# Linear attention and a gated FFN on one core: the first batch's q by casting loads, the remainder tile's product in quadrants, the third batch's sums three slots later

## The chip, the core and the metric

One core of a Trainium2 chip runs the kernel. TensorE (PE) multiplies, VectorE (DVE), ScalarE (ACT) and GpSimd (POOL) work element by element, and SyncE (SP), ACT and POOL issue transfers (DMAs). The metric is the device time of one execution in microseconds: the median of the runs.

## What is computed

```python
# attention part, per batch and head: q, k, v are (8 batches, 8 heads, 576 rows, 64)
kv = np.einsum('bhsd,bhse->bhde', k, v)
out = np.einsum('bhsd,bhde->bhse', q, kv)
rms = np.sqrt(np.mean(out * out, axis=-1, keepdims=True) + 1e-06)
attn = out / rms * g_norm
# FFN part on 4608 tokens of 512: w_gate, w_val (512, 1536), w_out (1536, 512)
x = attn.transpose(0, 2, 1, 3).reshape(4608, 512)
xn = x / np.sqrt(np.mean(x * x, axis=-1, keepdims=True) + 1e-06) * rms_g
g = xn @ w_gate
y = (g / (1 + np.exp(-g)) * (xn @ w_val)) @ w_out
```

All inputs and the output are float32; the kernel multiplies in bfloat16.

## The kernel before

Each batch has 576 rows. 512 of them are the main part, handled as four chunks of 128 (`MAIN`, `NC`); the 64 left over are the remainder (`REM`). Two batches' remainders form one tile of 128 rows, and the eight remainders together make one more token group of 512 for the FFN. So the FFN runs over nine groups of 512 tokens, in the order 0 to 6, the remainders, 7.

A group's FFN is a row of slots. A gate slot (`gate_of`, `mm1`) multiplies x by 128 columns of `w_gate` into a PSUM tile of the pool `mm1` (three buffers), and ACT takes its silu (line 703). A val slot does the same with `w_val`, and DVE multiplies it by the silu into h (line 712). After 12 pairs, the output slots (`slots_b`) multiply h by `w_out` into the PSUM pool `o2` (two buffers), ACT copies the tile to `osb` and SP stores it. Attention work of the next batch is laid between these slots. The PSUM pool `att` has three buffers.

Two ways set the order of the work. From the third batch on, a `Placer` walks the slots, and puts each operation into the first slot with room, by listed costs and by what it depends on (`place_attention`). Each engine then executes its instructions strictly in the order in which they stand. In `place_attention` PE makes kv and then o (`o_heads`: lines 367 to 378, 64-row matmuls that use the two row halves of the array); ACT squares o (`sq_`) and copies it (`outa_`); POOL multiplies the square by the squared gain (`wsq`); DVE sums both over each head (`red`, line 473), turns the sums into one factor per row and head (`chain`, twelve short steps) and scales the rows (`xna_`); SP transposes them to x by DMA (`x_dma`). The third, fourth, sixth and eighth batches also handle the remainder tile of two batches (`o_rem`, eight matmuls with 128 rows of weights, line 362).

The first batch, lines 820 to 996, is written out by hand. The loads: POOL issues loads that cast to bfloat16 on the way, first v (`load_cast`), then `w_gate` and `w_val` in four pieces each (`load_w`). A POOL load waits until the one eight before it has landed. SP and ACT issue plain loads: k in two halves of four heads, then q's first two chunks in 512-byte pieces. q's last two chunks are issued by SP and ACT behind the landing of v's remainder (line 838). DVE, ACT and POOL cast what came as float32 (`cast_main`).

The first half of the tokens (chunks 0 and 1) takes the shortest way. `kv_pairs` makes kv for two heads at a time (a pair, index j; `P0` are pairs 0 and 1, `P1` are 2 and 3) and DVE masks it (line 304). `qT_mm` transposes q on PE (line 316) and ACT and DVE copy it out (line 338). `oT_mm` (line 423) makes the transposed o, ACT squares it (line 434), `stat_pairs` sums the squares by matmul (line 448). `lead_chain` makes the factor: four DVE steps, a square root on ACT (line 497), the load of the silu table on ACT (line 498), a reciprocal on DVE (line 499). Meanwhile `o_pairs` makes o itself (line 390), DVE scales it (`xna_pairs`, line 400), PE transposes it (line 571), and ACT and DVE copy it to x with the gain (lines 581 and 583). Then come 22 early slots over these 256 tokens, `gates` (line 722) first. `spin` (line 245) fills PE's waits with matmuls on zeros.

`behind(n)` puts the second half's attention behind early slot n: transposes of q at 0, oT at 2 and 3, sums at 5, the chain at 5 to 9, o at 7 and 8, scaling at 11 and 12, transposes of x at 14 and 15. After 19 of the early slots, three slots over the second 256 tokens follow, and then the last three early ones.

Of the kernel before, what the change touches and what calls it, by code (L numbers as in the profile page):

```python
# [87 lines left out]
def kernel(  # L88
# [17 lines left out]
    NC = 4  # L106
# [17 lines left out]
    sq_p = pool("sq", 3)  # L124
# [64 lines left out]
    def load_cast(b, t, heads=None):  # L189
        to = qc if t == 0 else (vc if t == 2 else kc)[b % 2]  # L190
        if heads is None:
            if t == 0:
                to = q01r[b * REM : (b + 1) * REM]
            else:
                to = to[:REM, :, NC * D :]
            return nc.gpsimd.dma_start(
                out=to, in_=src[t][b, :, MAIN:S, :].rearrange("h p d -> p h d")
            )
        view = src[t][b, :, 0:MAIN, :].rearrange("h (p c) d -> p h (c d)", c=NC)[:, heads[0] : heads[1]]
        return nc.gpsimd.dma_start(out=to[:, heads[0] : heads[1], : NC * D], in_=view)  # L200

# [48 lines left out]
    class Att:  # L250
# [61 lines left out]
        def qT_mm(self, js, chunks, pool=None):  # L312
            qT_ps = (pool or att_p).tile([128, len(js), len(chunks) * 128], BF16, name="o2" if pool else "att")
            for n, j in enumerate(js):
                for i, c in enumerate(chunks):
                    nc.tensor.matmul(
                        qT_ps[:, n, i * 128 : (i + 1) * 128], lhsT=self.pair(0, c, j), rhs=ident, is_transpose=True,
                        start=True, stop=True, skip_group_check=True,
                    )
            return qT_ps  # L320
# [34 lines left out]
        def o_rem(self):  # L355

            self.o[NC] = o = att_p.tile([128, H, D], FP32, name="att")
            of = (kvs[2], kvs[1]) if self.b == 2 else (kvs[0], kvs[1])
            for j in range(NS):
                for n in range(2):  # L360
                    at = slice(n * REM, (n + 1) * REM)
                    nc.tensor.matmul(  # L362
                        o[at, 2 * j : 2 * j + 2, :], lhsT=self.qTj[:, j, NC, at], rhs=of[n][:, j, :, :],
                        start=True, stop=True, skip_group_check=True,
                    )

        def o_heads(self):

            for n, (pool_, name) in enumerate(((o2_p, "o2"), (o2_p, "o2"), (att_p, "att"), (att_p, "att"))):
                self.o["main", n] = pool_.tile([128, 2, H // 2, D], FP32, name=name)  # L370
            for c in range(NC):
                for j in range(NS):
                    for half in range(2):
                        rows = slice(half * D, (half + 1) * D)
                        nc.tensor.matmul(  # L375
                            self.o["main", c // 2 * 2 + half][:, c % 2, j, :], lhsT=self.qTj[rows, j, c, :],
                            rhs=self.kv[rows, j, half, :], start=True, stop=True, skip_group_check=True,
                        )

# [237 lines left out]
    def place_attention(P, b, casts=(), at=0, chain_at=0):  # L617
# [9 lines left out]
        main = P.psum(0.73, a.o_heads, kv + qt, 2)  # L627
        for c in N1:
            p = P.psum(0.3, a.o_rem, kv + qt) if c >= NC else main
            s = P.put("ACT", 0.6, lambda c=c: a.sq_(c), [p])  # L630
            outs[c] = P.put("ACT", 0.6, lambda c=c: a.outa_(c), [p])
            if c >= 2:
                P.tiles[-1 if c >= NC else c - 4] += [s, outs[c]]
# [99 lines left out]
    def rows_of(g, t):  # L733

        if g < B:
# [88 lines left out]
    v_loads = [G.dma_start(out=vr[: REM // 2].rearrange("p h c d -> p h (c d)"), in_=two(2))]  # L824
    v_loads += [load_cast(0, 2, hsx) for hsx in (H0, H1)]
    load_main(0, 1, H0)
    load_main(0, 1, H1, queue=A)
    load_main(0, 0, cs=(0, 2))
    krst = stage.tile([128, H, NC * D], FP32, name="stg")[: REM // 2, :, : 2 * D]
    A.dma_start(out=krst, in_=two(1))  # L830
# [5 lines left out]
    for hsx, queue in ((H0, nc.sync), (H1, A)):  # L836
        rest = load_main(0, 0, hsx, cs=(2, 4), queue=queue)
        tc.add_manual_dep(rest.ins, v_loads[0].ins.name, SYNC, reason="k and v have the queues first")

    make_identity(nc, ident)  # L840
    make_identity(nc, identf)
    w_loads = [load_w(n) for n in range(len(FB))]
    G.memset(kvs[0], 0.0)
    G.memset(kvs[1], 0.0)
    for tile_ in (kc[0], kc[1], vc[0], vc[1]):
        G.memset(tile_[REM:, :, NC * D :], 0.0)
# [7 lines left out]
    spin(mm1_p.tile([128, MAIN], FP32, name="mm1"), 18)  # L854
# [4 lines left out]
    cast_main(0, 0, V, cs=(0, 2))  # L859
    kva = a.kv_pairs(P0, 4)  # L860
    qa, qb = (a.qT_mm(js, (0, 1)) for js in (P0, P1))
    gT = o2_p.tile([128, NS + 1], FP32, name="o2")
    nc.tensor.matmul(gT, lhsT=grow, rhs=identf, is_transpose=True, start=True, stop=True, skip_group_check=True)
    kvb = a.kv_pairs(P1)
    for i, j in enumerate(P0):
        a.kv_pairs_out(kva, i, j)
    a.qT_out(qa, P0, 0, A)
    a.qT_out(qb, P1, 0, V)
# [5 lines left out]
    ta = a.oT_mm(P0, 0, 2, o2_p)  # L874
    a.sqT_(ta, P0, 0, 2)
    for i, j in enumerate(P1):
        a.kv_pairs_out(kvb, i, j)
# [3 lines left out]
    for i, j in enumerate(P1):  # L881
        a.sqT_(a.oT_mm((j,), 0, 2, (o2_p, mm1_p)[i], 4 * (1 - i)), (j,), 0, 2)
# [10 lines left out]
    for j, pool_, eng in zip(ALL, (o2_p, o2_p, None, None), (A, V, A, V)):  # L893
        a.xT_mm((j,), (0, 1), pool_)
        a.xT_out(j, (0, 1), eng)

    for hsx in (H0, H1):
        cast_main(0, 0, G, hsx, cs=(2, 4))
    for t in (0, 2, 1):
        load_cast(1, t, (0, H))  # L900
        if t:
            load_cast(1, t)
    wo_loads = [load_wo(n) for n in range(NF // OB)]
# [12 lines left out]
    steps = {5: (0, 4), 7: (4, 6), 8: (6, 8), 9: (8, 12)}  # L916

    def behind(n):
        if n == 0:
            ps = a.qT_mm(ALL, (2, 3))  # L920
            a.qT_out(ps[:, 0:2], P0, 2, V)
            a.qT_out(ps[:, 2:4], P1, 2, V)
        elif n in (2, 3):
            js = (P0, P1)[n - 2]
            a.sqT_(a.oT_mm(js, 2, 4, o2_p), js, 2, 4)
        elif n == 5:
# [6 lines left out]
        if n in (7, 8):  # L933
            held[n - 7] = a.o_pairs((P0, P1)[n - 7], 2, 4, att_p, "att")
        if n in (11, 12):
            i = (11, 12).index(n)
            a.xna_pairs(held[i], (P0, P1)[i], 2, 4)
        elif n in (14, 15):
            i = (14, 15).index(n)
# [47 lines left out]
    cut = len(early) - FB[-1]  # L987
# [37 lines left out]
```

## Time and profile before

| | us |
|---|---|
| median of 3 runs | 321.6 (321.56 to 321.62) |
| the profiled execution | 321.76 |
| its span, first to last instruction | 320.0 |
| PE busy in the span | 312.8 |
| DVE, ACT, POOL busy | 169.2, 138.0, 85.2 |

The profile shows the one execution that was traced; its own time stands 0.16 us above the median. Its page gives the busy time of each engine and the span in 40 slices of 8 us. PE's row of slices begins 8 7 9, and is 9 (90% or more) from there up to the last slice, where it is 5. Work on PE includes the filler matmuls, so a busy PE isn't always useful. Other views of the trace used below are the chain of work that ended last in order of time, the timeline of instructions (start, length, engine, line, operation, number of instructions, and in brackets the idle time before the first and what ended it), and windows, which give the busy time of each engine in a stretch and the bytes that the DMAs wrote.

### The profile page before, as it was taken

What the parts mean: (1) busy time and instruction counts of PE and PEld (TensorE: products, weight loads), DVE (VectorE), ACT (ScalarE), POOL (GpSimd) and SP (SyncE); (2) the same over time, 40 slices, a digit from 0 to 9 for tenths busy, and PEclk for the clock granted to TensorE, in tenths of its full rate; (3) what the DMA queues carried; (4) which work ended last, traced back from release to release, by engine and by line L of the source; (5) the groups of instructions that cost most, each with busy time, mean ns of one, the idle gap of its engine ahead of it and who ended that gap; (6) DMA issues with size and microseconds to landing.
All of it is one profiled execution on the core that took longest, in us unless ns stands there. A gap on an engine that the chain in (4) does not pass through costs nothing.

```text
span 320.0 us, 5497 instructions
## 1 busy us (share of the span) xinstructions
PE 312.8 (98%) x2122; PEld 157.7 (49%) x2122; DVE 169.2 (53%) x381; ACT 138.0 (43%) x254; POOL 85.2 (27%) x105
## 2 busy tenths in 40 slices
PE   8799999999999999999999999999999999999995
PEld 3578865444444444444544444444444444444443
DVE  4565536589749651955186717571778043203410
ACT  1465454596667314632383228322842233223321
POOL 8653430077017400830075007500510000000000
PEclk9999999999999999999999999999999999999999
DMA  8999999999761974498349875964000600040002
GB/s 210 221 203 199 195 231 205 228 209 135 153 197 53 166 155 137 131 166 153 121 128 133 148 153 145 153 127 137 11 3 10 183 21 2 15 107 12 0 33 98
DMA packets 79253, 40.69 MB, mean 127 GB/s; under 512 B 42872, under 2 KB 74748, under 8 KB 79228
## 3 DMA queue, kind: packets, MB, share of 16 engines
q0 software_dynamic: 31200, 14.22, 35.1%
q1 hardware_dynamic: 46544, 25.14, 32.2%
q10 hardware_dynamic: 1484, 0.99, 1.0%
q8 instruction: 16, 0.26, 0.3%
q14 instruction: 9, 0.07, 0.1%
HBM read 37.78 MB, written 9.44 MB: 148 GB/s over the span
## 4 chain that ended last, share of the span: by engine, by line
PE 91%; DMA 8%; issue 0%; DVE 0%; ACT 0%; POOLq 0%
PE mm L694 57%; PE o L729 27%; DMA wv<-in_moe_w_val_dram 5%; DMA remv<-in_v_dram 2%; PE att L281 2%; PE mm L729 2%; PE o L375 1%; PE att L375 0%; PE att L362 0%; PE mm L756 0%; PE o L756 0%; PE att L571 0%; PE att L327 0%; PE att L423 0%; PE att L350 0%
## 5 line engine op out<-in xcount | busy, mean ns | idle before, releaser
L712 DVE TENSOR_TENSOR h<-silu,mm 128x512 bf16<-128x512 bf16 (+1 forms) x120 | 75.5, 631 | 86.9 <-PE mm L694 77.0
L703 ACT ACTIVATE silu<-mm 128x512 bf16<-128x512 f32 (+1 forms) x120 | 66.4, 556 | 86.4 <-PE mm L694 75.3
L694 PE MATMUL mm<-x,wv 128*128 128x512 bf16 (+1 forms) x432 | 99.9, 356 | 0.2 <-DMA wv<-in_moe_w_val_dram 0.2
L694 PE MATMUL mm<-x,wg 128*128 128x512 bf16 (+1 forms) x420 | 97.9, 358 | 0.0
L729 PE MATMUL o<-wo,h 128*128 128x512 bf16 x396 | 90.1, 379 | 0.0
L694 PEld LDWEIGHTS <-wv 128*128 128x128 bf16 x480 | 46.2, 98 | 45.7 <-DMA wv<-in_moe_w_val_dram 0.5
L694 PEld LDWEIGHTS <-wg 128*128 128x128 bf16 x468 | 45.1, 98 | 45.7 <-DMA wg<-in_moe_w_gate_dram 0.2
L465 POOL TENSOR_TENSOR sq<-sq,g 128x512 bf16<-128x512 bf16 x28 | 32.0, 1154 | 129.0 <-ACT sq L410 129.0
L729 PEld LDWEIGHTS <-h 128*128 128x128 bf16 x420 | 40.3, 98 | 46.5
L745 ACT COPY osb<-o 128x512 f32<-128x512 f32 x33 | 19.3, 587 | 69.1 <-PE o L729 69.1
L473 DVE TENSOR_REDUCE st<-sq 128x8 f32<-128x512 bf16 x56 | 35.9, 678 | 0.2
L310 DVE CAST kvs<-att 64x256 bf16<-64x256 f32 x14 | 5.9, 422 | 31.9 <-PE att L281 31.7
L540 DVE TENSOR_TENSOR xna<-outa,al 128x512 bf16<-128x512 bf16 x24 | 15.0, 683 | 0.0
L694 PE MATMUL mm<-xr,wg 128*128 128x512 bf16 x48 | 12.3, 379 | 0.0
L694 PE MATMUL mm<-xr,wv 128*128 128x512 bf16 x48 | 12.3, 379 | 0.0
L216 POOL CAST main_q<-stg 128x1024 bf16<-128x1024 f32 (+1 forms) x12 | 11.4, 996 | 1.1 <-DMA stg<-in_q_dram 1.1
L245 PE MATMUL mm<-idle 128*128 128x512 bf16 x27 | 9.0, 505 | 1.2 <-DVE idle L138 1.2
L410 ACT ACTIVATE sq<-att 128x512 bf16<-128x512 f32 x16 | 9.8, 615 | 0.0
L414 ACT CAST outa<-att 128x512 bf16<-128x512 f32 x16 | 9.6, 600 | 0.0
L850 ACT ACTIVATE wv<-wv,gain 128x384 bf16<-128x384 bf16 x16 | 9.0, 608 | 0.4 <-PE mm L694 0.4
L200 POOL DMA_DIRECT2D vc<-in_v_dram x9 | 7.8, 872 | 1.1 <-PE mm L694 1.1
L729 PE MATMUL mm<-wo,h 128*128 128x512 bf16 x24 | 7.8, 379 | 0.0
(132 smaller groups left out, 175.1 us busy)
## 6 DMA issues: line engine op xcount, KB each, us to landing
out_dram<-osb SPq DMA_DIRECT2D x31, 256.0 KB, 2.5
stg<-in_q_dram SPq DMA_DIRECT2D x6, 1024.0 KB, 7.5
vc<-in_v_dram POOLq DMA_DIRECT2D x7, 512.0 KB, 8.2
kc<-in_k_dram POOLq DMA_DIRECT2D x7, 512.0 KB, 6.2
wg<-in_moe_w_gate_dram POOLq DMA_DIRECT2D x4, 384.0 KB, 14.9
wv<-in_moe_w_val_dram POOLq DMA_DIRECT2D x4, 384.0 KB, 16.3
wo<-in_moe_w_out_dram POOLq DMA_DIRECT2D x4, 384.0 KB, 14.7
out_dram<-osb SPq DMA_DIRECT2D x9, 128.0 KB, 2.3
```

The costliest lines, as they stand in the source:

```text
L216: return copy(out=mains[b, t][:, cs[0] : cs[1], h0:h1, :], in_=staged[b, t].rearrange("p h (c d) -> p c h d", c=NC)[:, cs[0] : cs[1], h0:h ...
L245: nc.tensor.matmul(ps, lhsT=idle[:, :128], rhs=idle[:, : ps.shape[-1]], start=True, stop=True, skip_group_check=True)
L410: nc.scalar.activation(out=self.sq[c][:, 0], in_=self.o_of(c), func=ACT.Square)
L414: nc.scalar.copy(out=self.outa[c], in_=self.o_of(c))
L465: eng.tensor_tensor(out=self.sq[c][:, 1], in0=self.sq[c][:, 0], in1=g2, op=OP.mult)
L473: nc.vector.reduce_sum(out=self.part(self.st[:, which], c), in_=of, axis=AX.X)
L540: return eng.tensor_tensor(out=self.part(self.xna, c), in0=self.outa[c].rearrange("p (c h) d -> p c h d", c=2), in1=self.part(self.al, c). ...
L694: nc.tensor.matmul(ps[:, : c1 - c0], lhsT=w[n][:, s, jj * 128 : (jj + 1) * 128], rhs=x_of(g, s, c0, c1), start=s == 0, stop=s == NS - 1)
L703: nc.scalar.activation(out=sis[g, j][:, c0:c1], in_=ps, func=ACT.Silu)
L712: nc.vector.tensor_tensor(out=hs[g, j][:, c0:c1], in0=sis[g, j][:, c0:c1], in1=v_ps, op=OP.mult)
L729: nc.tensor.matmul(ps, lhsT=hs[g, j][:, t * 128 : (t + 1) * 128], rhs=wo[j // OB][:, j % OB, :], start=j == 0, stop=j == NF - 1)
L745: (eng.copy if eng is nc.scalar else eng.tensor_copy)(out=o, in_=ps)
```

## The change

The first batch's q comes in four casting loads on POOL's queue, two for each half of the tokens, one for heads 0 to 3 into partitions 0 to 63 and one for heads 4 to 7 into partitions 64 to 127. A piece is 1024 bytes. The first two stand between the halves of v, of which the second is split in two; the other two stand behind v and behind the identity matrices, ahead of the weights. k comes in four quarters on SP and ACT, and k's remainder moves from ACT to SP. The float32 q loads and their casts are gone. The tokens' order inside the first batch changes with it, so that each of its output tiles is stored in two halves (`rows_of`). `qT_quads` transposes q in 64x64 pieces. kv of the pairs 2 and 3 is made one pair at a time.

The second half's q is transposed and copied out before the first gates, and its oT made there; the rest of its attention moves from early slots 5 to 15 to early slots 0 to 9. The three slots over the second 256 tokens stand after 13 early slots instead of 19. POOL's memsets of kvs, kc and vc move behind the loads of the second batch.

In the batches with a remainder tile, `o_rem` runs right behind `o_heads` as sixteen 64x64 matmuls into two PSUM tiles, one of `att` and one of `mm1`, for the even and the odd heads; ACT squares and copies each in halves, first of all chunks. For the third batch the DVE sums of the weighted squares are placed three slots later. The pool `sq` has four buffers instead of three.

```diff
+    def load_q0(part):
...
+        for hh in range(2):
+            nc.gpsimd.dma_start(
+                out=mains[0, 0][hh * D : (hh + 1) * D, part],
+                in_=q[0, hh * H // 2 : (hh + 1) * H // 2, part * MAIN // 2 : (part + 1) * MAIN // 2, :].rearrange(
+                    "h (p c) d -> p h (c d)", c=NC
+                ),
+            )
...
-        def qT_mm(self, js, chunks, pool=None):
...
+        def qT_quads(self, part, halves, pools):
+            tiles = [
+                pool.tile([128, 2, MAIN // 2], BF16, name="o2" if pool is o2_p else "att") for pool in pools
+            ]
+            for c in range(NC):
+                for h in range(H // 2):
+                    for ps, hh in zip(tiles, halves):
+                        rows, at = slice(hh * D, (hh + 1) * D), slice(h % 2 * D, (h % 2 + 1) * D)
+                        nc.tensor.matmul(
+                            ps[at, h // 2, c * D : (c + 1) * D],
+                            lhsT=mains[0, 0][rows, part, h, c * D : (c + 1) * D], rhs=ident[rows, rows],
+                            is_transpose=True, start=True, stop=True, skip_group_check=True,
+                        )
...
         def o_rem(self):
 
-            self.o[NC] = o = att_p.tile([128, H, D], FP32, name="att")
             of = (kvs[2], kvs[1]) if self.b == 2 else (kvs[0], kvs[1])
+            self.o[NC] = [
+                pool_.tile([128, H // 2, D], FP32, name=name) for pool_, name in ((att_p, "att"), (mm1_p, "mm1"))
+            ]
             for j in range(NS):
                 for n in range(2):
                     at = slice(n * REM, (n + 1) * REM)
-                    nc.tensor.matmul(
-                        o[at, 2 * j : 2 * j + 2, :], lhsT=self.qTj[:, j, NC, at], rhs=of[n][:, j, :, :],
-                        start=True, stop=True, skip_group_check=True,
-                    )
+                    for half in range(2):
+                        rows = slice(half * D, (half + 1) * D)
+                        nc.tensor.matmul(
+                            self.o[NC][half][at, j, :], lhsT=self.qTj[rows, j, NC, at],
+                            rhs=of[n][rows, j, half, :], start=True, stop=True, skip_group_check=True,
+                        )
...
+        rem = a.chunks - NC
+        main = P.psum(0.73 + 0.25 * rem, a.o_heads, kv + qt, 2 + rem)
+        for c in (*N1[NC:], *N1[:NC]):
+            if c == NC:
+                for n in (1, 0):
+                    s = P.put("ACT", 0.38, lambda n=n: a.sq_rem(n), [main])
+                    outs[c] = P.put("ACT", 0.38, lambda n=n: a.outa_rem(n), [main])
...
-            reds.append(P.put("DVE", 0.68, lambda c=c: a.red(c, 1), [w]))
+            reds.append(P.put("DVE", 0.68, lambda c=c: a.red(c, 1), [w], w[1] + 3 * (b == 2)))
...
+    load_cast(0, 2, H0)
+    load_q0(0)
+    load_cast(0, 2, (4, 6))
+    load_cast(0, 2, (6, 8))
+    for n, queue in enumerate((nc.sync, A, nc.sync, A)):
+        load_main(0, 1, (2 * n, 2 * n + 2), queue=queue)
...
+    load_q0(1)
     w_loads = [load_w(n) for n in range(len(FB))]
...
+    kva = a.kv_pairs(P0)
...
+    qa, qb = a.qT_quads(0, (0, 1), (att_p, att_p))
+    a.qT_out(qa, P0, 0, A)
+    a.qT_out(qb, P1, 0, V)
...
+    kvc = a.kv_pairs((2,))
+    ta = a.oT_mm(P0, 0, 2, o2_p)
...
+    kvd = a.kv_pairs((3,))
+    a.sqT_(a.oT_mm((2,), 0, 2, o2_p), (2,), 0, 2)
+    a.kv_pairs_out(kvd, 0, 3)
...
+    a.sqT_(a.oT_mm((3,), 0, 2, None, 2), (3,), 0, 2)
     a.stat_pairs(P0, 0, 2, mm1_p, "mm1", guard=True)
+    ox = a.o_pairs(P0, 0, 2, att_p, "att")
+    (la,) = a.qT_quads(1, (0,), (o2_p,))
+    a.qT_out(la, P0, 2, A)
     a.stat_pairs(P1, 0, 2, mm1_p, "mm1")
-    ox = a.o_pairs(P0, 0, 2, att_p, "att")
     oy = a.o_pairs(P1, 0, 2, att_p, "att")
+    (lb,) = a.qT_quads(1, (1,), (att_p,))
+    a.qT_out(lb, P1, 2, A)
     a.lead_chain(0, 2)
-    spin(mm1_p.tile([128, MAIN], FP32, name="mm1"), 5)
+    a.sqT_(a.oT_mm(P0, 2, 4, o2_p), P0, 2, 4)
+    xt = [a.xT_ps(1, (0, 1), pool_) for pool_ in (o2_p, o2_p, None, None)]
+    lo = a.oT_mm(P1, 2, 4)
+    spin(mm1_p.tile([128, MAIN], FP32, name="mm1"), 3)
...
+    for j in ALL:
+        a.xT_mm((j,), (0, 1), ps=xt[j])
+        a.xT_out(j, (0, 1), A if j == 2 else V)
+    a.sqT_(lo, P1, 2, 4)
...
-    steps = {5: (0, 4), 7: (4, 6), 8: (6, 8), 9: (8, 12)}
+    steps = {0: (0, 4), 1: (4, 6), 2: (6, 8), 3: (8, 12)}
...
-    cut = len(early) - FB[-1]
+    cut = 1 + 2 * FB[0] + FB[1] + FB[2]
```

More of the change, by code (lines that the diff above doesn't have):

```diff
@@ L123 @@
     outa_p = pool("outa", 6)
-    sq_p = pool("sq", 3)
+    sq_p = pool("sq", 4)
     stat = pool("stat", 2)
@@ L310, in kv_half @@
             nc.vector.tensor_copy(out=self.kv[rows, :, half, :], in_=self.kv_ps[rows, :, cols])
-        def qT_mm(self, js, chunks, pool=None):
[L313 to L317, printed above, removed]
-                        start=True, stop=True, skip_group_check=True,
-                    )
-            return qT_ps
+        def qT_quads(self, part, halves, pools):
[11 more added lines that the diff above has]
+                        )
+            return tiles
         def qT_heads(self, js, chunks):
@@ L733, in rows_of @@
     def rows_of(g, t):
+        if g == 0:
+            n = MAIN // 2
+            view = out[t // 2 * n : (t // 2 + 1) * n, :].rearrange("(p c) d -> p c d", c=NC)
+            return [(slice(i * D, (i + 1) * D), view[:, t % 2 * 2 + i, :]) for i in range(2)]
         if g < B:
@@ L823 @@
     ALL = range(NS)
[L824 to L828, printed above, removed]
+    G.dma_start(out=vr[: REM // 2].rearrange("p h c d -> p h (c d)"), in_=two(2))
+    load_cast(0, 2, H0)
[4 more added lines that the diff above has]
+        load_main(0, 1, (2 * n, 2 * n + 2), queue=queue)
     krst = stage.tile([128, H, NC * D], FP32, name="stg")[: REM // 2, :, : 2 * D]
-    A.dma_start(out=krst, in_=two(1))
+    nc.sync.dma_start(out=krst, in_=two(1))
     A.preload_act_table(ACT.Sqrt)
```

92 lines of the change are left out of this document (41 added, 51 removed).

## The prediction

> **What bounds the kernel now.** I read the page's busy shares, then the chain of waits in order of time, then the timeline of the first 32 us, and last the windows.
>
> ```profile
> PE 312.8 (98%) x2122; PEld 157.7 (49%) x2122; DVE 169.2 (53%) x381; ACT 138.0 (43%) x254; POOL 85.2 (27%) x105
> ```
>
> PE is nearly always busy, but filler counts as busy (27 spins of 512 columns, line 245). The chain shows where that matters:
>
> ```profile
> 1.31 7.23 DMA remv<-in_v_dram
> 8.54 0.28 issue
> 8.82 17.15 DMA wv<-in_moe_w_val_dram
> 25.98 0.05 issue
> 26.02 1.05 PE mm L694 x8
> ...
> 316.45 0.02 issue
> 316.47 0.27 ACT osb L764
> ```
>
> From 26 us on there is one unbroken run of PE work up to 316.45; before it, loads. So only three things move the end: when the first useful gate burst finishes, how much PE work lies behind it, and any hole in that run. The start:
>
> ```profile
> 9.07 1.04 ACT L216 CAST main_k<-stg 128x1024 bf16<-128x1024 f32 x1 [5.90 <-DMA remv<-in_v_dram]
> 10.43 0.38 PE L297 MATMUL mm<-vc,main_k 128*128 128x128 bf16 x4 [1.48 <-DMA vc<-in_v_dram]
> 11.52 0.59 ACT L338 COPY qTs<-att 128x512 bf16<-128x512 bf16 x1 [1.41 <-PE att L316]
> ...
> 14.42 0.26 DVE L491 RECIPROCAL r<-mm 128x16 f32<-128x16 f32 x1 [0.84 <-PE mm L448]
> 15.33 0.22 ACT L497 ACTIVATE nt<-z 128x16 f32<-128x16 f32 x1 [1.23 <-DVE z L494]
> 15.57 1.28 ACT L498 ACT_TABLE_LOAD   x1
> 15.58 0.25 DVE L499 RECIPROCAL al<-nt 128x16 f32<-128x16 f32 x1 [0.28 <-ACT nt L497]
> 15.95 1.42 DVE L400 TENSOR_TENSOR xna<-att,al 128x256 bf16<-128x256 f32 x4
> 17.54 1.47 PE L722 MATMUL mm<-x,wg 128*128 128x256 bf16 x12
> 18.84 0.94 ACT L703 ACTIVATE silu<-mm 128x256 bf16<-128x256 f32 x3 [0.95 <-PE mm L722]
> 18.85 0.61 PE L316 MATMUL att<-ident,main_q 128*128 128x128 bf16 x8
> ```
>
> PE waits 1.48 us for v; the chain of sums then runs 14.42 to 15.83 and the scaled rows (xna) to 17.37. The first gate burst ends at 18.84: call that G. Between G and 27.93, where the last hole closes, the instructions' own lengths (0.108 us per 256 columns) add to 8.5 of 9.1 us, so 0.6 us of holes.
>
> **The change, part by part.** The sum is made on the profiled execution: last PE work at 316.47, span 320.0, 321.76 in all, 0.16 above the median of 321.6.
>
> *Work taken out of the run behind G.* The second half's eight transposes of q (18.85 to 19.25, 0.40) and its four oT matmuls (20.17 to 20.39 and 20.83 to 21.05, 0.44) move ahead of G, into time where PE waits or spins. Gain 0.84. Uncovered, they cost it back, so 0 to 0.84.
>
> *Holes behind G.* The second half's sums now stand behind early slots 0 to 3 instead of 5 to 9. DVE gets 12 short steps (0.17 to 0.26 each), two xna of 0.65 and three h of 0.42 in a row, and PE's three mm1 buffers wait for those h. Laying these rows end to end from G: the sixth gate waits 0.36 for the third h, the q-side transposes 0.2 for xna, the seventh gate 0.13, some 0.1 elsewhere: 0.8, that is 0.2 more than now. Bounds: 0 more, or 1.0 more if ACT's x copies also hold silu back.
>
> *The remainder tile, four batches* (third, fourth, sixth, eighth). The stretch from gate to first output tile takes 21.85 us with it (90.67 to 112.52) and 21.40 without (123.73 to 145.13): 0.45 a tile for eight matmuls. The new sixteen are 64x64 quadrants like those of line 281, where 40 take 0.75, so 0.30: gain 0.15 each, 0.60 in all. The other bound is line 327's 1.01 for 32, which gives 0.51 each, a loss of 0.24. I take line 281, whose shape it is. ACT reads the tile in four pieces of 0.38 instead of 0.61 and 0.60, 0.3 more per tile; queued behind them is a silu, but between two silu ACT has 1.73 minus 0.60, and the pieces on the mm1 buffer come first, done some 0.8 us before PE wants that buffer. Priced at nothing; with that cover gone, up to 0.3 each.
>
> [...]
>
> *When G comes.* Casting queue first: it carries its first packet at 5.93 (the trace's packet records) and alone writes 198 GB/s (window 28 to 30). v's remainder (0.07 MB as written), v's first half and q's first half (0.26 each) need 2.98 us; the second half of v, 1.32 more; q's second half, another 1.32. From last packet to the waiting engine I take 0.8 (v's first half has its semaphores at 9.90 and PE goes at 10.43, some 0.3 more lies ahead of the semaphore), and 0.1 for k's remainder beside it. So q's first half is seen at 9.8, v at 11.1, q's second half at 12.4. Now q's first half shares with v through other queues (297 GB/s in 4 to 8), v's end is seen at 11.8.
>
> PE then: kv of the first two pairs ends 9.2 (0.66); 32 quadrant transposes at 19 ns, 9.8 to 10.4; ACT's copy 0.59, to 11.1; oT, to 11.5; kv of the last pair starts at 11.5 (now 11.79). ACT squares 0.55, 0.38, 0.38 in a row, to 13.0. Meanwhile PE does the first pairs' sums, o (0.23) and sixteen one-sided transposes; these share their row half, so 0.30 to 0.51, I take 0.4. The last sums end 13.6, and DVE has z at 14.5 (0.88, as 14.42 to 15.30).
>
> Here is the new wait: ACT must copy both q halves out first (0.59 each); the second is transposed by 14.25, so ACT is free at 14.95, not 14.5. Queued behind: nt, al, the table load. nt runs to 15.2, al to 15.45, xna to 16.97 (1.42). Table load to 16.5, then the square of the second half to 17.05, which frees the o2 buffer that the second x transpose needs. The x copies on DVE (0.35 each) then gate the burst: 17.35, 17.7, 18.05, ACT's at 17.8; with three matmuls (0.33) per copy the burst ends at 18.7. Gain 0.14. Bounds: with the one-sided transposes at 19 ns and an earlier copy 18.3, and 18.0 if the first casting packet comes 0.3 sooner (its place right behind k's packets leaves that open); with casting at half that rate for q, or 1 us later, 19.9.
>
> *Costed at nothing.* ACT's k cast no longer waits for v's remainder (hidden: before 10.6 only filler reads k's second half). Weights start at 11.8 instead of 10.95, but no longer share with q's second half: at 1.94 us a piece the fifth lands about 22.2, wanted at G + 5.9 = 24.6. If that cover went, each us late is a us lost. POOL's memsets behind the loads delay w_out's issue, which still has more than 5 us of queue before it. Batch 0's stores become eight instead of four, 2 us more on SP ahead of the fourth batch's q load (61.39, 7.5 to land, cast at 75.0). The third batch's sums: laid out, its last x transpose is issued at 86.3 behind a store and lands 89.5 (3.2), wanted at 90.5; now it is 3 us early, so 1 us of slack remains, and its last h comes 0.6 before PE wants it at 81.8.
>
> Sum: -0.84 + 0.2 - 0.60 - 0.14 = -1.38. PE ends at 315.1, the execution takes 320.4, the median **320.2 us**.
>
> **The rivals.**
>
> *q lands late.* Everything in the lead hangs on one queue. For it: its first packet comes only when k's have gone, and pieces now go to 64 partitions at a time. Against it: 198 GB/s for the same 512-byte writes. At half rate for q the first half comes 1.3 later, G is 20.0, the sum -0.1: 321.5.
>
> *The quadrants give nothing*: transposes and remainder at line 327's 32 ns. Against it: line 281. The remainder costs 0.24 instead of gaining 0.60, the lead 0.5 more: sum 0, 321.6. [...]
>
> *PE slows down in the lead; slower.* The first spins take 0.43 per 512 columns, and 0.216 only after some 6 us (line 245's starts 2.03, 2.46, ..., 7.06). The new lead has fewer spins (27 to 21) and more short waits between 8 and 17. If these put PE back to 0.43, the burst takes 2.6 instead of 1.3 and the dense work behind it twice as long for another 2 to 3 us: +2.9, sum +1.5, 323.1. Against it: a pause of 1.48 (8.95 to 10.43) costs nothing now, while my longest is 0.8. It decides once a pause, or the loose stretch, passes what 1.48 has been shown to bear.
>
> *A late third batch.* If its x misses 90.5, PE stands there for the lateness; 0.7 late gives 320.9, and slower than now needs 3 late.
>
> **How the numbers follow.** Forecast 0.60 (its own range 319.3 to 320.9); q late 0.14 (321.5); quadrants give nothing 0.10 (321.6, half of it nearer the 25 ns result); third batch late 0.06; PE slow or several losses at once 0.10 (323). What a measurement tells from no change is 0.2%, 0.64 us. Faster (below 320.96): the forecast, half of the quadrant case, half of the late batch, 0.68. Same: the late q, less a third, and the rest of these two, 0.17. Slower: the slow PE and that third, 0.15. The range runs from 319.3 (G at 18.0 and no hole more than now: 0.9 better than the forecast) to 322.2, which leaves out most of the slow case.
>
> **What would show it.** G near 18.7 with nt waiting for ACT's copy and the second x transpose for ACT; no wait for weights; some 0.8 us of holes after G; 40 + 16 quadrants at 18 to 19 ns, and 21.7 us for the fourth batch's stretch. Wrong if q's first half is seen after 10.5, if spins or gates in 12 to 20 take 0.43 per 512 columns, or if PE waits anywhere after 30 us.

## The result and the profile after

The changed kernel takes 320.26 us (median of 13 runs, 319.64 to 321.71), the kernel before 322.0 us beside it (13 runs, 321.56 to 322.8). The ratio is 0.9949, with a 95% interval of 0.9937 to 0.996. The forecast was 320.2. The profiled execution took 319.64 us, with a span of 317.8.

Busy time on the page:

```profile
PE 309.3 (97%) x2176; PEld 157.5 (50%) x2198; DVE 168.0 (53%) x379; ACT 139.5 (44%) x263; POOL 87.3 (27%) x108
```

PE has 54 instructions more and is busy for 3.5 us less: there are fewer fillers, and quadrants share their time (sixteen take 0.25 us, below). The chain of waits, in order of time (start, length, what):

```profile
4.05 6.29 DMA vc<-in_v_dram
...
15.11 1.28 ACT L532
...
16.40 0.61 ACT sqT L468
...
17.55 1.16 PE mm L762 x10
...
24.14 11.48 PE mm L734 x104
...
313.09 1.32 PE mm L800 x12
314.41 0.02 issue
314.44 0.28 ACT osb L808
```

Before, the chain ran over a load of weights that ended at 25.98. Now it follows a piece of v (heads 4 and 5, seen at 10.34; the last piece comes at 11.25), the sums, the silu table on ACT and the square behind it, and from the first gates at 17.38 PE has no hole over 0.16 us. PE's work ends at 314.41 instead of 316.45. Rows of the lead, from the timeline of all engines:

```profile
8.54 0.38 PE L310 MATMUL mm<-vc,main_k 128*128 128x128 bf16 x4 [0.64 <-DMA vc<-in_v_dram]
9.70 0.44 PE L333 MATMUL att<-ident,main_q 64*64 64x64 bf16 x31 [0.18 <-DMA main_q<-in_q_dram]
11.25 0.23 PEld L310 LDWEIGHTS <-main_k 128*128 128x128 bf16 x4 [0.32 <-DMA vc<-in_v_dram]
13.77 0.26 DVE L525 RECIPROCAL r<-mm 128x16 f32<-128x16 f32 x1 [1.28 <-PE mm L482]
14.39 0.59 ACT L356 COPY qTs<-att 128x512 bf16<-128x512 bf16 x1 [0.21 <-PE att L333]
14.87 0.22 ACT L531 ACTIVATE nt<-z 128x16 f32<-128x16 f32 x1
15.41 1.42 DVE L434 TENSOR_TENSOR xna<-att,al 128x256 bf16<-128x256 f32 x4
17.05 0.27 PE L605 MATMUL o<-ident,xna 128*128 128x128 bf16 x2 [0.87 <-ACT sqT L468]
17.38 1.52 PE L762 MATMUL mm<-x,wg 128*128 128x256 bf16 x12
18.73 0.94 ACT L743 ACTIVATE silu<-mm 128x256 bf16<-128x256 f32 x3 [0.29 <-PE mm L762]
```

The waits that the prediction named are there: nt stands right behind ACT's second copy of q, and the second x transpose waits 0.87 us for ACT's square.

To see where the 2.04 us come from, cut PE's time at four instants: the last v's arrival (its kv products start), G (the first silu starts), T (the second batch's q is transposed) and E (the last output tile starts, with its first weight load).

| stretch, us | before | after | difference | forecast |
|---|---|---|---|---|
| start to G | 18.84 | 18.73 | -0.11 | -0.14 |
| G to T | 17.93 | 16.82 | -1.11 | -0.84 + 0.2 |
| T to E | 276.66 | 275.85 | -0.81 | -0.60 |

The sum is -2.03, where -1.38 was forecast. The medians differ by 1.74 only, since the traced execution is the fastest of the 13, 0.62 us under their median. Its last v came rather early (11.25 us, where the other traces of the same loads have 10.97 to 11.95), and the time goes with it: v at 10.97, 11.25 and 11.71 stands beside 319.37, 319.64 and 320.05 us in three traces: the changed kernel with the old cut, as it is, and with more filler. Executions with a lower granted clock, of which more below, don't explain the smaller difference: the changed kernel has 3 of 13 at 0.993, and of the kernel before five of 13 took 322.58 us or more, times that go with 0.995 in its runs beside the experiments.

### The profile page after: what moved, and what is told of

Its sections match the earlier page's. It is cut to its first block, busy times and chain, and to the rows that moved or that the text cites. A ratio compares the mean times of both kernels' runs of the same rounds, so it can differ in the third digit from the quotient of the medians.

```text
span 317.8 us, 5653 instructions
## 1 busy us (share of the span) xinstructions
PE 309.3 (97%) x2176; PEld 157.5 (50%) x2198; DVE 168.0 (53%) x379; ACT 139.5 (44%) x263; POOL 87.3 (27%) x108
## 4 chain that ended last, share of the span: by engine, by line
PE 94%; DMA 2%; ACT 1%; issue 1%; POOL 1%; DVE 0%; POOLq 0%
PE mm L734 59%; PE o L769 27%; DMA vc<-in_v_dram 2%; PE att L294 2%; PE mm L769 2%; PE o L407 1%; PE att L407 0%; PE att L605 0%; PE mm L800 0%; PE o L800 0%; ACT L532 0%; PE mm L762 0%; PE att L457 0%; PE mm L310 0%; PE att L345 0%
## 5 line engine op out<-in xcount | busy, mean ns | idle before, releaser
L769 PE MATMUL o<-wo,h 128*128 128x512 bf16 x382 | 87.7, 379 | 1.1 <-issue 0.6
L229 POOL CAST main_q<-stg 128x1024 bf16<-128x1024 f32 x10 | 10.3, 1074 | 0.0
L200 POOL DMA_DIRECT2D vc<-in_v_dram x10 | 8.6, 862 | 3.5 <-DMA wv<-in_moe_w_val_dram 2.4
L258 PE MATMUL mm<-idle 128*128 128x512 bf16 x20 | 6.9, 512 | 1.3 <-DVE idle L138 1.2
L444 ACT ACTIVATE sq<-att 128x512 bf16<-128x512 f32 x12 | 7.6, 630 | 0.0
L444 ACT ACTIVATE sq<-o 128x512 bf16<-128x512 f32 x12 | 7.3, 610 | 0.0
```

The source lines that it names most:

```text
L229: return copy(out=mains[b, t][:, cs[0] : cs[1], h0:h1, :], in_=staged[b, t].rearrange("p h (c d) -> p c h d", c=NC)[:, cs[0] : cs[1], h0:h ...
L444: nc.scalar.activation(out=self.sq[c][:, 0], in_=self.o_of(c), func=ACT.Square)
L769: nc.tensor.matmul(ps, lhsT=hs[g, j][:, t * 128 : (t + 1) * 128], rhs=wo[j // OB][:, j % OB, :], start=j == 0, stop=j == NF - 1)
```

## The experiments

All times are medians; the ratio is to the kernel before, with its interval. Each diff is against the changed kernel, unless it says otherwise.

### One whole remainder tile at the new place

```diff
-            self.o[NC] = [
-                pool_.tile([128, H // 2, D], FP32, name=name) for pool_, name in ((att_p, "att"), (mm1_p, "mm1"))
-            ]
+            whole = att_p.tile([128, H, D], FP32, name="att")
+            self.o[NC] = [whole[:, half:H:2, :] for half in range(2)]
...
+                    nc.tensor.matmul(
+                        whole[at, 2 * j : 2 * j + 2, :], lhsT=self.qTj[:, j, NC, at], rhs=of[n][:, j, :, :],
```

> The changed kernel with the remainder tile's product in eight full-height matmuls again, but at its new place right behind the main chunks' product, in one tile of att, read by ACT in the same halves. Theory (the quadrants' shape is the gain): each of the four remainder tiles costs 0.15 to 0.2 more PE time, 0.6 to 0.8 in all, the end of PE work near 315.1. Rival A (the place is the gain: one switch between kinds of matmul fewer): 0 to 0.05 more each, the end within 0.2 of 314.4. Rival B (the piece in mm1 holds gates up): the end comes earlier than 314.4.

320.43 us, 0.9957 (0.9942 to 0.9973). T to E is 276.24, and PE has no wait between T and E in this trace or in the one before: of the 0.81 us that the remainder tile brings, 0.39 (0.10 a tile) go with the shape, and 0.42 stay with the place, right behind other 64-row matmuls instead of on its own between 128-row ones. That it is the change of the array's shape that costs there wasn't tried by itself. In the kernel before, the chain of waits has the fourth batch's tile on its own:

```profile
93.83 0.97 PE mm L694 x4
94.80 0.34 PE att L362 x8
95.14 17.37 PE mm L694 x80
```

What PE does at the new place is in the changed kernel's timeline:

```profile
91.76 0.41 PE L407 MATMUL o<-kvs,qTs 64*128 64x64 bf16 x16
92.01 0.40 PE L407 MATMUL att<-kvs,qTs 64*128 64x64 bf16 x16
92.33 0.21 PE L384 MATMUL att<-kvs,qTs 64*64 64x64 bf16 x1
...
92.58 1.04 PE L734 MATMUL mm<-x,wv 128*128 128x512 bf16 x4
```

Sixteen quadrants take 0.25 us, from 92.33 to 92.58.

### The third batch's sums not later

```diff
-            reds.append(P.put("DVE", 0.68, lambda c=c: a.red(c, 1), [w], w[1] + 3 * (b == 2)))
+            reds.append(P.put("DVE", 0.68, lambda c=c: a.red(c, 1), [w], w[1]))
```

> The changed kernel with the third batch's sums of the weighted squares where the placer puts them without the three slots. Theory (they are off the path, in time either way): the end of PE work within 0.1 of 314.4; the third batch's x lands up to 2 us earlier. Rival (the three slots keep POOL's late squares from holding DVE's h): PE has a hole between 62 and 82 us, 0.2 to 1 us.

321.26 us, 0.9982 (0.997 to 0.9995). T to E is 277.07: 1.22 us more, all of it inside the third batch's stretch. Rows of its timeline there:

```profile
69.14 0.69 POOL L196 DMA_DIRECT2D kc<-in_k_dram  x1
69.83 1.17 POOL L499 TENSOR_TENSOR sq<-sq,g 128x512 bf16<-128x512 bf16 x1
71.04 0.69 DVE L507 TENSOR_REDUCE st<-sq 128x8 f32<-128x512 bf16 x1 [0.88 <-POOL sq L499]
71.64 0.68 DVE L752 TENSOR_TENSOR h<-silu,mm 128x512 bf16<-128x512 bf16 x1
72.37 1.02 PE L734 MATMUL mm<-x,wg 128*128 128x512 bf16 x4 [0.85 <-DVE h L752]
```

POOL issues two loads ahead of the weighted square, the square ends at 71.0, and DVE's sum stands at the head of its queue and waits 0.88 us for it. The h behind the sum is ready to run and can't; PE wants h's buffer and waits 0.85 us. With the sums three slots later DVE has h first (71.35 to 72.03 in the changed kernel) and no such wait:

```profile
71.35 0.68 DVE L752 TENSOR_TENSOR h<-silu,mm 128x512 bf16<-128x512 bf16 x1
```

The kernel before, which has no shift, has no hole here either. From its chain of waits:

```profile
67.26 12.19 PE mm L694 x56
```

So the shift wins nothing over the kernel before; it keeps the rest of the change from losing 1.22 us. That it is the new order of the remainder tile which makes it necessary is likely, but no run tried that by itself.

### The second half of q turned behind the gates again

```diff
-    (la,) = a.qT_quads(1, (0,), (o2_p,))
-    a.qT_out(la, P0, 2, A)
...
-    (lb,) = a.qT_quads(1, (1,), (att_p,))
-    a.qT_out(lb, P1, 2, A)
...
-    steps = {0: (0, 4), 1: (4, 6), 2: (6, 8), 3: (8, 12)}
+    steps = {4: (0, 4), 5: (4, 6), 6: (6, 8), 7: (8, 12)}
...
+            for ps, js in zip(a.qT_quads(1, (0, 1), (att_p, att_p)), (P0, P1)):
+                a.qT_out(ps, js, 2, V)
+        elif n in (2, 3):
+            js = (P0, P1)[n - 2]
+            a.sqT_(a.oT_mm(js, 2, 4, o2_p), js, 2, 4)
```

> The changed kernel with one part undone: the second half's q is turned, copied and multiplied to oT behind the first gates again, and its sums and scaling stand two to four early slots later. Theory (an earlier turn takes work out of the run behind the gates, but pays for it ahead of them): the first gate burst ends 0.5 earlier than the changed kernel's 18.73, near 18.2, since the root no longer waits for ACT's second copy and the second x transpose no longer for ACT's square; behind it stand 0.84 of PE work more; the last PE work comes 0.3 later than the changed kernel's 314.4, near 314.7, and the time is some 0.3 us above it. Rival A (the whole 0.84 is gain): the burst ends at 18.7 as before and the end is at 315.3 or later. Rival B (the early turn is a loss): the end is before 314.4.

321.34 us (321.01 to 324.32), 0.9989 (0.9972 to 1.0007). The traced execution, 323.52 us with a granted clock of 0.994, was one of two long ones out of twelve, so the comparison was made again with more filler in the lead, the same that the run behind it adds to the changed kernel:

```diff
-    for _ in range(4):
+    for _ in range(8):
...
-    kvc = a.kv_pairs((2,))
+    kvc = a.kv_pairs((2,), wait=1)
...
-    kvd = a.kv_pairs((3,))
+    kvd = a.kv_pairs((3,), wait=1)
```

> Second half of q turned behind the gates again, with the same added filler. The look at the earlier run without it had a stretch at clock 0.50 from 10.9 to 14.2 us in it, and PE holes of 0.82 and 0.85 us behind DVE's h and xna. Queue theory: turning late costs by itself, since the second pair of chunks' sums then start 3.3 us later and meet h on DVE: 321.0 to 321.4 at clock 1.0, with these holes in the trace. Clock theory: the loss was the half clock alone: 320.0 to 320.4, no hole over 0.4 us behind 18 us.

> The changed kernel with more idle matmuls in the lead: eight instead of four behind k's cast (ahead of the first v), and one of 512 columns ahead of each of the last two v pieces' products. Clock theory: a stretch of about 3.4 us in which PE is little busy is followed by one of 3.4 us at half clock; in 3 of 13 runs of the changed kernel (granted clock 0.993, 320.89 to 321.71 us) this happened once. With more filler no run has a clock under 0.997, the longest run stays under 320.9, and the median is 319.9 to 320.2. Rival: the long runs come from v arriving late, and the filler only takes its place in PE's queue: the longest run stays near 321.5, median 320.3 to 320.6.

Late with filler: 321.25 us (320.92 to 321.85), 0.9973 (0.9962 to 0.9983). Early with filler: 320.05 us (319.8 to 322.3), 0.9942 (0.9923 to 0.9961). Turning early is worth 1.20 us, and it isn't the clock, which was 0.998 to 1.0 in all executions of the late one. From the late one's timeline:

```profile
21.22 0.17 DVE L546 TENSOR_SCALAR u<-att 128x16 f32<-128x16 f32 x1 [0.67 <-PE att L482]
24.02 0.69 DVE L434 TENSOR_TENSOR xna<-att,al 128x512 bf16<-128x512 f32 x1
24.77 0.40 PE L605 MATMUL o<-ident,xna 128*128 128x128 bf16 x4 [0.49 <-DVE xna L434]
```

The second half's sums start 3.39 us behind G (17.83) instead of 0.39 (19.12 and 18.73), and PE waits for the scaled rows. G to T takes 19.07 us instead of 16.82. But the lead is shorter: from v's arrival to G 6.50 us instead of 7.46 in the early one, since ACT has no second copies ahead of nt and no square ahead of the x copies. So the early turn costs 0.96 ahead of G and brings 2.25 behind it, both against the late order of this run. That order isn't the kernel before's, whose sums and scaling stand later still: there G to T takes 17.93, 1.14 less than here. The holes came out smaller than the 0.82 and 0.85 expected; those belong to the disturbed execution (clock 0.994).

### No filler in the lead

```diff
-    for _ in range(4):
-        nc.tensor.matmul(
-            idle_ps[:, : 4 * D], lhsT=idle[:, :128], rhs=kh, start=True, stop=True, skip_group_check=True
-        )
...
-    a.sqT_(a.oT_mm((3,), 0, 2, None, 2), (3,), 0, 2)
+    a.sqT_(a.oT_mm((3,), 0, 2), (3,), 0, 2)
...
-    spin(mm1_p.tile([128, MAIN], FP32, name="mm1"), 3)
```

> The changed kernel without the nine filler matmuls that stand behind the first eighteen (four on k, two of 256 columns, three of 512). Theory (pauses of the length that this lead has don't slow PE): matmuls of 256 columns in 12 to 20 us keep their 0.108 us, the first gate burst ends within 0.1 of 18.73, the end of PE work within 0.15 of 314.4. Rival (filler keeps PE's speed up): the spacing in the burst goes to some 0.21 per 256 columns, the burst ends 1.3 later, and the time is 1 to 3 us above the changed kernel's.

322.25 us (321.05 to 323.95), 1.0013 (0.9992 to 1.0034): 2 us lost by leaving out work that computes nothing. All twelve executions had a granted clock under 1 (0.977 to 0.995). The windows of its trace are cut at steps of 3.375 us from the moment (4.07) at which the first spins go from 0.43 to 0.22 us apart. The columns are the stretch and its length, the busy time of PE, PE's weight loads, DVE, ACT and POOL, then the granted clock, the DMA share and GB/s:

```profile
7.45:10.82 3.37, 1.65 (x48) 1.38 (x48) 1.29 (x4) 0.19 (x1) 2.88 (x5) 1.00 1.42 188
10.82:14.20 3.38, 3.21 (x26) 2.31 (x24) 1.37 (x7) 1.76 (x4) 3.27 (x5) 0.51 1.35 200
14.20:17.57 3.37, 3.15 (x47) 1.84 (x44) 1.30 (x6) 1.86 (x4) 1.72 (x2) 0.50 1.31 203
17.57:20.95 3.38, 2.42 (x15) 1.88 (x16) 2.10 (x7) 2.26 (x4) 0.73 (x2) 0.50 1.32 203
20.95:24.32 3.37, 3.37 (x26) 2.50 (x25) 1.60 (x8) 0.94 (x3) 2.03 (x4) 0.50 1.32 203
```

PE is busy for 1.65 of 3.37 us in the first window, and the clock is 0.5 in the next. It stays there for four windows, also behind those in which PE is busy for 3.21 and 3.15; only after one that is full is it 1.0 again. The gate burst falls inside: from its first matmul to the first silu it takes 2.4 us (19.52 to 21.90) instead of 1.35. The longest pause of PE there is 1.79 us.

The step of 3.375 us is an estimate and a little short. In this trace the clock falls at 10.89 and comes back at 24.55, 13.66 later; in the disturbed execution with q turned late it falls at 10.87 and comes back at 14.29, 3.42 later; with q by plain loads, the run after this one, it falls at 11.81 and comes back at 15.22, 3.41 later. The first time is four times the other two, within 0.02. In the first two the fall comes 6.82 and 6.81 behind the change of the spins, twice 3.41. At steps of 3.41 from 4.07 on, the five windows hold 1.73, 3.24, 3.05, 2.60 and 3.41 us of PE work, which reads the same.

The same cut through the disturbed execution with q turned late, whose spins change at 4.06:

```profile
7.43:10.81 3.38, 1.86 (x50) 1.41 (x48) 1.25 (x4) 0.14 (x1) 2.80 (x5) 1.00 1.43 190
10.81:14.18 3.37, 3.37 (x27) 2.60 (x27) 1.43 (x7) 1.81 (x4) 3.36 (x5) 0.51 1.34 198
```

And through the kernel before, whose spins change at 6.97:

```profile
6.97:10.34 3.37, 1.98 (x9) 0.78 (x8) 0.78 (x2) 1.04 (x1) 2.00 (x3) 1.00 1.35 212
10.34:13.72 3.38, 3.29 (x43) 2.88 (x42) 2.75 (x10) 1.41 (x3) 2.59 (x5) 1.00 1.30 217
```

Here 1.86 goes with a fall and 1.98 with none. If the change of the spins marks where a step begins, that differs from one execution to the next: it comes at 4.06 with q turned late, at 5.70 in the changed kernel and at 6.97 here. The changed kernel's lowest windows, at steps of 3.41, have 2.77 and 2.46, and its clock stays at 1.0. But the sum of PE's work alone doesn't decide. The same disturbed execution has, behind its gates:

```profile
25.90 0.60 PE L734 MATMUL mm<-x,wg 128*128 128x256 bf16 x4 [0.82 <-DVE h L752]
...
27.34 0.40 PE L605 MATMUL o<-ident,xna 128*128 128x128 bf16 x4 [0.85 <-DVE xna L434]
```

Its window from 24.53 to 27.94 holds 1.74 us of PE work, less than the 1.89 of the one that fell (7.46 to 10.87, at the same step), and the clock stays at 1.0 behind it. What else counts isn't shown; the two windows above that fell hold 48 and 50 matmuls, most of them short, and the two that held have 9 and 18. Nor does the longest pause of PE decide: ahead of the fall it was 1.79 us in the trace without filler and 1.04 in the disturbed one, and in the kernel before one of 1.48 us went by without a fall.

### q by plain loads and casts, in the same pieces

```diff
-            nc.gpsimd.dma_start(
-                out=mains[0, 0][hh * D : (hh + 1) * D, part],
+        for hh, queue in enumerate((nc.sync, nc.scalar)):
+            queue.dma_start(
+                out=q_staged[0][hh * D : (hh + 1) * D, part],
...
+    V.tensor_copy(out=mains[0, 0][:, 0], in_=q_staged[0][:, 0])
+    G.tensor_copy(out=mains[0, 0][:, 1], in_=q_staged[0][:, 1])
```

> The changed kernel with the same four pieces of q by plain loads on SP and ACT behind k, cast by DVE (first half) and POOL (second). Theory (casting in the load saves the cast and its wait, and the one queue keeps its rate): v's end is seen near 11.8 instead of 11.25, q's first half is cast near 10.9 and turned 1 us later than now, the second half cast by POOL only near 14 to 15; the burst ends 1 to 2 us later than 18.73, and the time is 1 to 2 us above the changed kernel's. Rival (all loads share the same engines, who issues them doesn't matter, and the casts lie beside other work): within 0.5 us of it.

324.89 us, 1.0094 (1.0077 to 1.011), and G is 22.82. Its timeline shows where the time goes:

```profile
10.49 0.68 DVE L903 CAST remk<-stg 32x1024 bf16<-32x1024 f32 x1 [5.08 <-DMA stg<-in_k_dram]
11.61 0.43 PE L315 MATMUL mm<-vc,main_k 128*128 128x128 bf16 x4 [3.12 <-DMA vc<-in_v_dram]
```

q is written as float32, twice the bytes, and beside v and k's remainder: even v's first half comes 3.1 us later than in the changed kernel (8.54), the last v at 14.63 instead of 11.25. In the pause PE is busy for 0.27 us of the window from 8.38 to 11.76, its clock is then 0.50 from 11.81 to 15.22, and v's arrival to G takes 8.19 instead of 7.47.

### The second group's slots after 19 early slots again

```diff
-    cut = 1 + 2 * FB[0] + FB[1] + FB[2]
+    cut = len(early) - FB[-1]
```

> The changed kernel with the three slots over the second 256 tokens behind 19 early slots instead of 13, which wants the third piece of w_val and the fourth of w_gate 2.6 us earlier. Theory (weights are no bound any more: the third w_val piece is there 0.8 before it would be wanted, the fourth w_gate piece 1.2): no wait for weights, the end of PE work within 0.1 of 314.4. Rival (weights still bound the lead, as the chain of waits of before says with its 17 us on a weight load): a wait for a weight load between 24 and 28 us of 0.3 or more, and the end that much later.

320.14 us, 0.9948 (0.9929 to 0.9967); G to T 16.85 us. The cut changes nothing, and PE waits for no weights with either.

### Towards a faster version

First, o's second-half tile in the `mm1` pool, so that the second x transpose no longer waits for its square:

```diff
-    a.sqT_(a.oT_mm(P0, 2, 4, o2_p), P0, 2, 4)
+    a.sqT_(a.oT_mm(P0, 2, 4, mm1_p), P0, 2, 4)
```

> The changed kernel, with the second half's first oT in a buffer of mm1 instead of o2, so that the second x transpose has no buffer to wait for. Theory (that wait is 0.87 of the lead, but ACT's x copy of the third pair still stands behind the square): the second transpose starts right behind the second scaling, near 16.3 instead of 17.05; DVE's x copies run 16.75 to 17.75; ACT's ends 17.5; the burst ends 0.25 earlier, near 18.5, and the end of PE work comes 0.2 to 0.3 earlier than 314.4. Rival A (the wait is hidden behind the x copies on DVE): no change, within 0.1. Rival B (the third gate now waits for the mm1 buffer): the burst ends later than 18.8.

320.34 us, 0.9952 (0.9935 to 0.9968). From v's arrival to G it takes 7.17 us instead of 7.47, as the freed wait promised, but this kernel's v came at 11.95 in the trace, and two of six executions had a granted clock of 0.993, so the median doesn't show the gain. Then also ACT's square root ahead of its second copy of q, and all x copies on DVE:

```diff
-        def lead_chain(self, c0, c1, guard=False):
+        def lead_chain(self, c0, c1, guard=False, before_table=None):
...
+            if before_table:
+                before_table()
...
-    a.qT_out(lb, P1, 2, A)
-    a.lead_chain(0, 2)
+    a.lead_chain(0, 2, before_table=lambda: a.qT_out(lb, P1, 2, A))
...
-        a.xT_out(j, (0, 1), A if j == 2 else V)
+        a.xT_out(j, (0, 1), V)
```

> As e7_free_o2, and ACT takes the root ahead of its second copy of q, and DVE makes all four x copies. Theory (the new wait that the prediction named is ACT's second copy before the root): the root starts with z, near 14.67 instead of 14.87, the scaling ends 0.2 earlier, DVE's four x copies end near 17.95, the burst ends near 18.3, and the end of PE work is 0.35 to 0.45 earlier than 314.4, some 0.12% faster than the changed kernel. Rival (ACT or the squares decide behind the gates): the gain of the burst is lost again in holes before 24 us, end within 0.15 of 314.4.

319.59 us (319.37 to 320.1), 0.9929 (0.9916 to 0.9942), 0.2% better than the changed kernel by the medians, with intervals that overlap a little. From v to G 7.15 us: al comes sooner, four x copies in a row on DVE take it back. So the next kernel gives the third x copy back to ACT and has the added filler:

> The root ahead of the second copy and o's tile of its own (319.59 us), with the added filler and the third x copy given to ACT again, so that DVE has three in a row and not four. Theory: first silu 0.1 to 0.3 us nearer to v's arrival than 7.15 us; 319.2 to 319.5, all clocks over 0.997. Rival: ACT is at its squares then, x comes as late as on DVE: 319.5 to 319.8.

319.76 us (319.49 to 320.97), 0.9927 (0.9909 to 0.9945), 7.13 us from v to G: the rival is right, ACT is at its square until 17.62 and ends the copy no sooner. The last one moves the first x copy to ACT ahead of the square, and the filler into PE's longest wait:

```diff
-    spin(mm1_p.tile([128, MAIN], FP32, name="mm1"), 3)
+    spin(mm1_p.tile([128, MAIN], FP32, name="mm1"), 4)
...
-        a.xT_out(j, (0, 1), A if j == 2 else V)
+        a.xT_out(j, (0, 1), V if j else A)
+    a.sqT_(lp, P0, 2, 4)
```

> As the run before, but the four idle matmuls stand in PE's wait for ACT's second copy of q (0.75 us) instead of ahead of the x transposes, ACT copies the first x right behind its table load, and its square of the second half's first pairs comes after that. Theory: x is then complete 0.2 us sooner, the first silu 6.9 to 7.0 us behind v's arrival (7.14 and 7.15 in the two runs before), 319.3 to 319.6 us, and every window of 3.4 us in the lead has PE busy for more than 2.5, so that no run has a clock under 0.997. Rival: the squares come later on ACT by as much, and the second half's sums hold PE behind the first gates instead: 319.6 to 320.0, with a hole at the sums (line 482).

319.88 us (319.73 to 320.06), 0.9936 (0.9921 to 0.9951), 7.50 us from v to G. The rival is right, at another place than it said. The trace has:

```profile
17.21 0.59 ACT L468 ACTIVATE sqT<-mm 128x512 bf16<-128x512 f32 x1
17.37 1.74 PE L764 MATMUL mm<-x,wg 128*128 128x256 bf16 x12 [0.23 <-ACT x L617]
```

The first two gates start at 17.37 and 17.48, the third only at 17.85: its `mm1` buffer is the one that ACT's square (to 17.80) still reads. On the clock this run went as expected: the windows of 3.41 us have 3.00 us or more of PE work, and all six executions had a granted clock of 1.0. The runs with added filler in the early part alone had one of nine (322.3 us, clock 0.995), one of six (320.97, 0.995) and none of eleven, so the clock theory's "no run" was wrong for that filler. In the changed kernel it is 3 of 13 (320.89 to 321.71, 0.993), in the kernel before 5 of 11 beside this run (322.38 to 322.63, 0.995, against 321.46 to 321.75 for its others). Six executions are too few to call that cured.

## Why the prediction was right, and where not

**The number.** The median, 320.26, lies 0.06 from the forecast 320.2, and that closeness is in part luck. The traced execution took 319.64 where the sum gave 320.38, so the gain was larger than forecast by 0.74. The forecast then took off 0.16 for the median, which lies 0.62 above the trace instead. The two misses cancel. The stretches below show which terms of the sum held.

**G.** Forecast 18.7, measured 18.73, by the steps given: v's first half 8.5 (8.54), q 9.8 (9.70), the last v 11.1 (11.25), the last sums 13.6 (13.77), nt behind ACT's second copy at 14.95 (14.87), xna's end 16.97 (16.83), the second x transpose 17.05 (17.05). Two inputs were off and cancelled: the casting queue's first packet came at 4.98, not 5.93 (in the trace before it stands at 5.80, a little ahead of what the forecast read), and from 6 to 11 us 188 GB/s were written, not 198. The quadrant transposes were mis-sized too: 31 start within 0.37 us, 12 ns apiece, where both row halves are used; 16 of one half take 0.37, 23 ns.

**Work taken out behind G.** -0.84 + 0.2 was forecast, -1.11 measured, so the holes shrank by 0.27 and didn't grow by 0.2. The step that failed is laying the rows end to end: DVE's lengths overlap. In the changed kernel DVE starts h (0.42 long) at 20.53 and the next step at 20.87, 0.34 later, and the short steps of 0.17 cost about 0.2. PE waited for no h. The runs with q turned late say more than the forecast did: against their order the move is worth 2.25 behind G and costs 0.96 ahead of it. The forecast had that cost inside G, as nt's new wait.

**The remainder tile.** 0.15 a tile was forecast, 0.20 measured, and only half of it comes by the step that the forecast gave. The shape brings 0.10; the new place brings the other 0.10, and the forecast had no term for that. The quadrants themselves were priced too high: the first matmuls of four start within 0.02 us of each other, and sixteen take 0.25 and not 0.30. That is 15.6 ns apiece. The 25 ns in the sentence on the chances is in no run: beside the 15.6, the lead has 12 ns where both row halves are used and 23 where one is.

**Costed at nothing.** Weights, k's cast and the stores were hidden, as said: no wait in the trace, and the old cut changes nothing. The third batch's shift was judged by its x alone, as slack given away, and that is harmless indeed. What it keeps was missed: without it the change would lose 1.22 us of its 2.03 again. The reading that would have found it asks of each sum which POOL square it waits for, and which h stands behind it on DVE. k in four quarters, the later memsets and the fourth buffer of `sq` were not undone by themselves, so what they cost or bring isn't shown.

**The rivals.** *q late* did not come; the plain loads show the cost of a late lead, 4.1 us at G. *The quadrants give nothing* is refuted by 0.25 us for sixteen. *A late third batch* did not come. *PE slow in the lead* was the best of them: without the filler the clock was 0.50 for 13.66 us, the burst took 2.4 us, and the median was 2 us longer. The forecast held against it that a pause of 1.48 us costs nothing before; but it isn't the longest pause that decides, since the clock fell in an execution whose longest pause ahead of the fall was 1.04. The falls came behind windows with little PE work (1.73 and 1.89 us of 3.41, and 0.27 of 3.38 with plain loads), but 1.74 elsewhere had none. By that measure the change moved a little away from the fall: the least busy 3.41 us of the lead, at any phase, hold 1.93 us of PE work in the trace before and 2.13 in the changed kernel's. Which window the 3 of 13 executions lost is open, since none of them was traced.

## What to carry to other kernels

On a stretch in which PE waits often, sum its busy time over windows as long as the traces show the clock to stay down, 3.41 us here, before moving work. Here the clock fell to 0.50 behind windows with 51% and 55%, and 95% did not bring it back; but one with 51% elsewhere let it stand, so a low sum is a warning and not a rule. A DVE sum that waited 0.88 us for its input here held up the h behind it, and through that PE for 0.85, so a step that is "later" can be what saves the gain of a change. When work moves ahead of the critical burst, price both ends: against one late order, early turning cost 0.96 us in the lead to win 2.25 behind it.

## What the runs showed of the hardware

In the three traces with a fall (no filler, q turned late, q by plain loads), the granted clock went from 1.00 to 0.50 at 10.89, 10.87 and 11.81, and was back at 1.00 after 13.66, 3.42 and 3.41 us. Ahead of each fall stood a window with a low share of PE work (1.73 and 1.89 us of 3.41, and 0.27 of 3.38), but one with 1.74 of 3.41 behind the gates had no fall behind it, so the rule by which it falls stays open.

One short DVE step, the int32 TENSOR_SCALAR of the second half's chain, is 0.17 us long in the changed kernel. In three traces in which it fell beside POOL's memsets of `kvs` (q turned late, no filler, q by plain loads) it took 1.51, 0.88 and 1.14 us, and each time it ended 0.03 us behind the second memset's end. With q turned late and no added filler that is 1.34 us more, and G to T is 1.33 us longer (20.40) than with filler (19.07), where the step ended before the memsets began. No run was made to take the memsets away, so the cause is argued and not shown.

The last v's arrival differs from trace to trace by up to 1 us (10.97 to 11.95) with the same loads in the same order, which is as large as most of what was tried in the lead.
